# Output product in two row tiles with a drain per chunk, column-tile work gathered in one stretch, MLP work spread over head pairs

## The chip, the cores and the metric

One core of one Trainium2 chip. The metric is device time in microseconds (us), the median of several executions; the profiler took one execution of each kernel. "Span" is the profiled execution's time from its first to its last instruction; it is about 2 us shorter than the device time. A run is called slow when it is over 1.5% above the fastest of its kernel, else fast. Ratios use fast runs alone; a median that includes a slow run is marked.

## The reference

```python
# q, k, v: (8, 12, 448, 64) float32
scores = q @ k.T / 8 - log(448)
attn   = sigmoid(scores)                  # no softmax
x      = (attn @ v) -> (8, 448, 768)
wq, wk = x @ w_q, x @ w_k                 # 768 -> 64
mixed  = (wq @ wk.T / 8) @ x              # token mixing; the kernel does wq @ (wk.T @ x)
out    = relu(mixed) @ w_out              # (8, 448, 768) float32
```

## The kernel before

The unit of work is a "head pair" `n`: two batches and two heads (`u` is the batch pair, `j` the head pair in it; 4 x 6 = 24 pairs). ScalarE has seven sigmoids of 128 x 896 per pair. TensorE transposes q, k and x, makes scores and value products, and carries the MLP of the batch pair before along with it. The order inside a pair is written by hand:

```python
    for n, (u, j) in enumerate(pairs):
        ...                                   # loads, casts
        left = {0: 2, 1: 1}.get(j, 2 * (NJ - j) + (2 if u < NU - 1 else 0))
        tr_q(n + 1)                           # column tiles (128 rows x 64 columns)
        scores_last(n)                        # column tiles
        tr_k(n + 1)                           # column tiles
        tr_x(n - 2)                           # column tiles
        if u > 0 and j == 1:
            mlp_wkn(u - 1)
        scores(n, 0); scores(n, 1)            # row tiles (64 rows x 128 columns)
        whole(left)                           # output chunks, the whole 128 x 128 array
        scores(n, 2); scores(n, 3)            # row tiles
        values(n - 1, 0); values(n - 1, 1)    # column tiles
        if u > 0 and j == 1:
            mlp_tmp(u - 1)
        scores(n, 4); scores(n, 5)            # row tiles
        if u > 0 and j == 0:
            mlp_wqk(u - 1)
        elif u > 0 and j == 1:
            for c in range(NC):
                mlp_mix(u - 1, c)
            outs += outs_of(u - 1)            # 14 chunks
        else:
            whole(left - 1)
```

An output chunk is six accumulating matmuls over the whole array, then one copy out of PSUM:

```python
    def mlp_out(u, m, nb):
        ps = ps_f.tile([P, NB], F32, tag="f", name="po")       # NB = 384
        for c in range(NC):                                    # NC = 6
            nc.tensor.matmul(
                ps, mxs[u][c]...[:, m * P : (m + 1) * P],
                wout16[:, c, nb * NB : (nb + 1) * NB],
                start=(c == 0), stop=(c == NC - 1),
            )
        nc.vector.tensor_copy(out=ot[0][:, nb * NB : (nb + 1) * NB], in_=ps)
```

PSUM: two score tiles of two banks each, and four single banks ("f") for everything else.

## Time and profile before

| | before |
|---|---|
| device time, median (lowest to highest of 3) | 250.95 us (250.38 to 251.14) |
| span | 248.5 us |
| busy: TensorE / ScalarE / VectorE | 87% / 69% / 53% |
| mean granted TensorE clock | 0.981 |
| first sigmoid starts | 9.7 us |
| first stage ends (first sigmoid of pair 6) | 52.8 us |
| last sigmoid ends | 219.2 us |

### The profile page before, as it was taken

The numbers are of one execution on the slowest core, as the hardware profiler recorded it, in microseconds if no ns is written. First come the engines' busy times: TensorE is split into PE (matmuls) and PEld (weight loads), VectorE is DVE, ScalarE is ACT, GpSimd is POOL, SyncE is SP. The second block draws the span as 40 slices with busy tenths as digits, with TensorE's granted clock in tenths as the row PEclk, the third lists the DMA queues.
The fourth block names the chain that finished last, engine by engine and source line by source line (L and its number), as shares of the span: only waits on it lengthen the run. The fifth ranks groups of instructions, "written<-read, shape, count | busy, mean of one in ns | idle before, by whom it ended". The sixth has DMA issues, their size and how long they took to land.

```text
span 248.5 us, 6124 instructions
## 1 busy us (share of the span) xinstructions
PE 215.9 (87%) x2480; PEld 116.7 (47%) x2480; DVE 132.2 (53%) x230; ACT 171.7 (69%) x194; POOL 75.5 (30%) x84
## 2 busy tenths in 40 slices
PE   0878777779779999999979999999979999998992
PEld 0534334445435644545544554455444554453660
DVE  2423444454575555564685654655684564458551
ACT  2499889986677768986688678895698678724000
POOL 1655466566302131441633041343631010000000
PEclk9979999999979999999999999999999999999997
DMA  6999999999900498789872489789962543220376
GB/s 239 303 286 268 249 330 318 308 296 262 247 2 21 115 275 231 187 231 286 224 216 65 114 240 263 211 234 259 234 170 66 130 105 95 67 63 3 79 201 163
DMA packets 35387, 47.58 MB, mean 191 GB/s; under 512 B 6432, under 2 KB 31008, under 8 KB 35360
## 3 DMA queue, kind: packets, MB, share of 16 engines
q1 hardware_dynamic: 35088, 46.74, 70.2%
q8 instruction: 19, 0.31, 0.6%
q10 hardware_dynamic: 272, 0.46, 0.5%
q14 instruction: 8, 0.07, 0.1%
HBM read 36.18 MB, written 11.01 MB: 190 GB/s over the span
## 4 chain that ended last, share of the span: by engine, by line
PE 72%; ACT 17%; issue 5%; DVE 2%; DMA 2%; ACTq 0%
PE po L289 19%; PE pv L203 16%; ACT at L169 15%; PE sc L187 12%; PE ptk L155 5%; PE ptq L139 5%; PE sc L177 5%; PE px L223 4%; PE pw L236 4%; ACT mx L280 2%; PE pt L263 2%; DMA q<-in_q_dram 2%; PE pm L275 1%; DVE tmp L268 1%; PE pk L251 1%
## 5 line engine op out<-in xcount | busy, mean ns | idle before, releaser
L169 ACT ACTIVATE at<-sc,bias_t 128x896 bf16<-128x896 f32 x168 | 158.8, 1006 | 49.3 <-PE sc L177 23.7
L289 PE MATMUL po<-wout,mx 128*128 128x384 bf16 x336 | 59.6, 327 | 0.1
L187 PE MATMUL sc<-qt,kt 64*128 64x448 bf16 x288 | 47.2, 358 | 14.4 <-ACT at L169 14.0
L294 DVE COPY o<-po 128x384 f32<-128x384 f32 x56 | 31.2, 558 | 37.7 <-PE po L289 36.6
L207 DVE CAST xt<-pv 128x448 bf16<-128x448 f32 x48 | 30.0, 625 | 39.6 <-PE pv L203 36.4
L289 PEld LDWEIGHTS <-mx 128*128 128x128 bf16 x336 | 30.6, 98 | 25.2 <-issue 7.2
L203 PE MATMUL pv<-at,v 128*64 128x448 bf16 x384 | 40.9, 356 | 0.0
L116 POOL CAST q<-q 128x896 bf16<-128x896 f32 x23 | 21.5, 933 | 59.0 <-DMA q<-in_q_dram 29.9
L125 POOL CAST v<-v 128x1024 bf16<-128x1024 f32 x24 | 25.0, 1040 | 38.4 <-PE pv L203 21.0
L187 PEld LDWEIGHTS <-kt 64*128 64x128 bf16 x288 | 12.3, 93 | 43.3 <-issue 40.8
L116 POOL CAST k<-k 128x896 bf16<-128x896 f32 x24 | 22.6, 940 | 24.5 <-DMA k<-in_k_dram 16.9
L203 PEld LDWEIGHTS <-v 128*64 128x64 bf16 x384 | 19.7, 109 | 17.0 <-issue 6.1
L159 DVE COPY kt<-ptk 128x1024 bf16<-128x1024 bf16 x24 | 16.6, 690 | 9.7 <-PE ptk L155 9.7
L139 PE MATMUL ptq<-ident,q 128*64 128x128 bf16 x336 | 15.5, 238 | 6.0 <-DVE q L116 6.0
L143 DVE COPY qt<-ptq 128x896 bf16<-128x896 bf16 x24 | 15.0, 624 | 8.6 <-PE ptq L139 8.5
L139 PEld LDWEIGHTS <-q 128*64 128x64 bf16 x336 | 11.3, 119 | 14.2 <-issue 6.5
L280 ACT ACTIVATE mx<-pm 128x448 bf16<-128x448 f32 x24 | 11.7, 550 | 8.1 <-PE pm L275 8.0
L155 PEld LDWEIGHTS <-k 128*64 128x64 bf16 x336 | 15.1, 120 | 4.2 <-issue 0.8
L224 DVE COPY xn<-px 128x1024 bf16<-128x1024 bf16 x24 | 16.4, 681 | 0.4 <-PE px L223 0.4
L177 PE MATMUL sc<-qt,kt 128*64 128x448 bf16 x96 | 14.5, 382 | 2.2 <-ACT at L169 2.2
L155 PE MATMUL ptk<-ident,k 128*64 128x128 bf16 x336 | 16.4, 233 | 0.0
L279 DVE TENSOR_SCALAR mx<-pm 128x448 bf16<-128x448 f32 x24 | 13.8, 619 | 2.6 <-PE pm L275 2.4
(36 smaller groups left out, 125.5 us busy)
## 6 DMA issues: line engine op xcount, KB each, us to landing
q<-in_q_dram SPq DMA_DIRECT2D x24, 448.0 KB, 5.9
out_dram<-o SPq DMA_DIRECT2D x56, 192.0 KB, 2.7
k<-in_k_dram SPq DMA_DIRECT2D x23, 448.0 KB, 7.0
v<-in_v_dram SPq DMA_DIRECT2D x48, 128.0 KB, 6.0
v<-in_v_dram SPq DMA_DIRECT2D x48, 96.0 KB, 5.6
w<-in_moe_w_out_dram SPq DMA_DIRECT2D x6, 384.0 KB, 6.2
k<-in_k_dram ACTq DMA_DIRECT2D x1, 448.0 KB, 4.9
wqk<-in_moe_w_q_dram SPq DMA_DIRECT2D x2, 192.0 KB, 6.4
```

The source lines that it names most:

```text
L116: eng.tensor_copy(out=t16.rearrange("p b i d -> p b (i d)"), in_=ld.pop((nm, n)))
L125: nc.gpsimd.tensor_copy(out=t.rearrange("p b h s d -> p (b h s d)"), in_=v32[n % NV].rearrange("p b h s d -> p (b h s d)"),)
L139: nc.tensor.transpose(ps[HALF[b2], i].rearrange("p h n -> p (h n)"), t16[:, b2, i, :], ident16)
L155: nc.tensor.transpose(ps[HALF[b2], pos].rearrange("p h n -> p (h n)"), src, ident16)
L169: nc.scalar.activation(at, sc[:, :, 0:S], ACTF.Sigmoid, bias=bias_t, scale=attn_scale)
L177: nc.tensor.matmul(sc[HALF[b2], h, 0:S], kts[n][:, h, 3 * P + 64 * b2 : 3 * P + 64 * b2 + 64], qts[n][:, h, :], start=True, stop=True,)
L187: nc.tensor.matmul(sc[:, b2, 0:S], kts[n][HALF[b2], h, m * P : (m + 1) * P], qts[n][HALF[b2], h, :], start=True, stop=True,)
L203: nc.tensor.matmul(ps[HALF[b2]], v16s[n][:, b2, h, slot, :], rhs, start=(m == 0), stop=(m == 3))
L207: nc.vector.tensor_copy(out=t, in_=ps)
L280: nc.scalar.activation(mxs[u][c][:, 1, :], ps[1], ACTF.Relu, bias=0.0, scale=moe_scale)
L289: nc.tensor.matmul(ps, mxs[u][c].rearrange("p b s -> p (b s)")[:, m * P : (m + 1) * P], wout16[:, c, nb * NB : (nb + 1) * NB], start=(c == ...
L294: nc.vector.tensor_copy(out=ot[0][:, nb * NB : (nb + 1) * NB], in_=ps)
```

## The change

The intent: score matmuls use TensorE in two row tiles of 64 rows. If the output product does so too, scores and output can alternate without a change of tiling mode, in small "slots" between the score tiles. All work in column tiles is gathered in one stretch at the start of a pair, so a pair changes mode twice and not seven times. Upper and lower half of a chunk add into the same PSUM bank, so the upper half runs seven slots behind the lower one and a drain stands between them. The mix steps of the MLP are spread over three head pairs. The head of the program (warm-up matmuls, casts and copies in halves) and the tail (`wqk` begun early, copies shared with ScalarE) are reworked too. The diff is shortened: `...` marks cuts, and guards such as `if n > 0` and the placing of the small MLP transposes are left out.

```diff
+    LAG = NC + 1
+    def out_mm(n, c, x, last):                      # x: 0 lower half, 1 upper half
+        if x == 0 and c == 0:
+            state[n] = bank([P, NB], F32, "po")
+        r = HALF[x]
+        if x == 1 and c == 0:
+            nc.tensor.drain()
+        nc.tensor.matmul(
+            state[n][1], mxs[u][c]...[r, m * P : (m + 1) * P],
+            wout16[r, c, nb * NB : (nb + 1) * NB],
+            start=(x == 0 and c == 0), stop=(x == 1 and c == NC - 1),
+        )
...
+    def out_slot(last=False):
+        if s < end:
+            out_mm(s // NC, s % NC, 0, last)
+        if 0 <= s - LAG < end:
+            out_mm((s - LAG) // NC, (s - LAG) % NC, 1, last)
...
+        tr_q(n + 1); tr_k(n + 1)
+        scores_last(n)
+        values(n - 1, 0); values(n - 1, 1)
+        tr_x(n - 2)
...
+        mixes = ((1, (0, 1, 2, 3, 4, 5)),) if u == 1 else ((1, (0, 1)), (2, (2, 3)), (3, (4, 5)))
...
+        if u == 0:
+            for g in range(first, 6):
+                scores(n, g)
+            continue
+        scores(n, 0)
+        scores(n, 1)
+        gaps = [5, 5, 4, 4]
+        for g in range(2, 6):
+            fill(todo, gaps[g - 2])                  # slots, wqk or mix steps
+            scores(n, g)
```

## The prediction

> **What bounds the kernel now.** I read the busy slices first, then the chain of work that ended last, in order of time, then the timeline of TensorE, and last the groups by line. The page's busy rows, in 40 slices of 6.2 us:
>
> ```profile
> PE   0878777779779999999979999999979999998992
> ACT  2499889986677768986688678895698678724000
> ```
>
> There are three stages. Up to about 52 us (the six head pairs of the first batch pair) ScalarE is the fuller engine. From 52 to 218 us TensorE is at nine tenths or more. From 218 us TensorE works alone. The chain gives each stage its price. A pair of the first stage, one of the second, and the tail:
>
> ```profile
> 30.43 0.57 PE sc L177 x4
> 37.65 0.57 PE sc L177 x4
> ...
> 83.21 0.51 PE ptq L139 x14
> 84.55 0.45 PE px L223 x16
> 84.99 0.63 PE sc L187 x4
> 85.62 2.06 PE po L289 x12
> 87.68 0.48 PE sc L187 x4
> 88.17 1.64 PE pv L203 x16
> 89.80 0.60 PE sc L187 x4
> 90.40 2.06 PE po L289 x12
> 92.46 0.51 PE ptq L139 x14
> ...
> 220.58 2.42 PE pw L236 x24
> 229.85 13.82 PE po L289 x84
> 243.70 0.56 DVE o L294
> ```
>
> The first two lines are the same work one pair apart: 37.65 - 30.43 = 7.22 us. The pair from 83.21 to 92.46 takes 9.25 us and is TensorE from end to end. The output product of the last batch pair is 84 matmuls in 13.82 us, 0.1645 each, just over the 0.160 us that 384 columns take when 448 take 0.187 (the 24 matmuls of `pw`, below). From the same chain I took the starts of all pairs: a batch pair of the steady stage (107.75 to 162.63 us) costs 54.9 us, as 8.8, 12.25, 9.25, 9.25, 7.65, 7.65. Eighteen pairs run from 52.1 to 218.5 us: 166.4. The tail takes 30 us, of which 11.35 come before the first output product and 4.8 after the last.
>
> ScalarE, in the timeline of the first stage:
>
> ```profile
> 29.38 6.56 ACT L169 ACTIVATE at<-sc,bias_t 128x896 bf16<-128x896 f32 x7 [0.65 <-PE sc L187]
> 34.49 1.70 PE L203 MATMUL pv<-at,v 128*64 128x448 bf16 x16
> 36.12 0.55 PE L187 MATMUL sc<-qt,kt 64*128 64x448 bf16 x4
> 36.59 1.91 ACT L169 ACTIVATE at<-sc,bias_t 128x896 bf16<-128x896 f32 x2 [0.65 <-PE sc L187]
> ```
>
> Two sigmoids take 1.91 and one takes 1.01 us, so a sigmoid follows the other after 0.90 us, and seven need 6.3 us. The hole of 0.65 us is the value product: 1.7 us of TensorE during which only two score tiles, all that its buffers hold, can wait for ScalarE.
>
> **What the Trainium skill says.** (1) "TensorEngine Tiling (Array Packing)", Key Properties: "Changing tiling mode (not just tile) drains the TensorE". The trace agrees and gives the size: four score matmuls in row tiles are 2 x 0.187 = 0.37 us but cost 0.48 after the output product, the value product is 8 x 0.187 = 1.50 but costs 1.64, 14 transposes are 0.39 but cost 0.51. A change of mode is 0.11 to 0.14 us. (2) The same page, Gotcha 1: different row tiles may not access one PSUM bank simultaneously. That is why the upper half of an output chunk must come after the lower; no run here shows what happens otherwise. (3) "TensorE: Matmul & The Clock Gate", Part 3, row and column tiling: matmuls in different row groups run concurrently. Agrees: the 24 `pw` matmuls, two row tiles in turns, took 2.27 us in the body's chain, 0.189 a pair. (4) "PSUM — Partial Sum Buffer", Engine vs sequencer instructions: a drain waits until the engine is fully idle. The trace has TensorE's closing drain: it ends at 243.71, when VectorE's last copy starts (243.70); the last matmul started at 243.34 and streamed for 0.16 until 243.50. So a drain holds for at least 0.21 us beyond the stream.
>
> **The change part by part.**
>
> *Row tiles for the output.* One 128-row matmul of 384 columns becomes two of 64 rows in two row tiles. They run side by side, so a slot (one lower, one upper) is about 0.162 us: TensorE time neither gained nor lost, 336 matmuls more. The gain is that output and scores share one mode. Before, a pair with four output chunks changes mode seven times, afterwards twice: 5 x 0.12 = 0.6 us.
>
> *The drain.* There are 56, one per chunk. Each lets the array empty (0.21 us, above) and the next weights and matmul be issued from an empty queue, which I put at 0.07: D = 0.28 us, an estimate. The two lanes pair up again after it (upper k with lower k+1), so nothing else is lost. Three chunks per pair: 0.84 us, more than the 0.6 saved.
>
> *One column stretch.* TensorE in a pair: transposes 0.51 + 0.45 + 0.45, last scores 0.375, values 1.50 = 3.28 us; about 0.1 for banks, because two of the four are held by open output chunks; change of mode 0.12; six score tiles 6 x 0.187 = 1.12. Sum 4.6. With 18 slots: 4.6 + 18 x 0.162 + 0.84 = 8.4 to 8.5. But ScalarE now has one hole per pair: from the last score tile, values (1.5), a transpose (0.45), a mode change (0.12) and one score pair with its latency (0.36) lie before the next, 2.43 us, of which two sigmoids less the start cover about 1.1. So a pair bound by ScalarE takes 6.3 + 1.35 = 7.65 to 7.8, not 7.2.
>
> *Spread of the slots.* I counted in the built order. Pairs 8 to 11, 16, 17, 22, 23 hold (about) 18 slots; 12 and 18 hold 6 and the `pw` work; 14, 15 and 21 few or none but two mix steps (0.9 us of ScalarE); 36 of the last-but-one batch pair's 84 are done when the body ends. So 48 + 7 slots stand in the tail, where ScalarE has nothing to do. Before, none were left.
>
> *Pair 1 of each batch pair.* The small transposes of `wqk` now come first, right behind the copies of `pw`: TensorE stands about 1.2 us, then works through 5 us of column tiles over two free banks. I get 6.9 us before the first score, then 5: 11.7 to 12.3, like 12.25 before.
>
> *Head.* Warm-up matmuls, k cast by two engines, halves of the copies: first sigmoid at about 7.9 rather than 9.68; but the second pair's k lands and is cast as late as before (9.5), and it now stands ahead of the last scores of pair 0. Gain 1.3 us.
>
> Sum: head -1.3. Five pairs without MLP, +0.45 each: +2.2. Body: 7.8 + 12.3 + 8 x 8.45 + 2 x 8.2 + 11.7 + 12.1 + 3 x 8.65 + 8.9 = 162.8 against 166.4: -3.6. Tail: 55 + 91 slots x 0.162 + 23 drains x 0.28 = 30.1 against 13.8: +16.3; `wqk` begun early and copies shared with ScalarE -1.4; shorter last transfer -0.4. Total 250.95 - 1.3 + 2.2 - 3.6 + 14.5 = 262.8. Some drains will fall into waits for ScalarE or a bank and cost nothing; I take 2 to 4 us off: 259.
>
> **The rivals.**
>
> *The drain is cheap* (0.12, as a mode change): 56 x 0.16 = 9 us less, 250 to 254, no change. For it: the array empties at a mode change too, for 0.12. Against it: the closing drain's 0.21[...].
>
> *The even spread pays.* If pairs of 18 slots run at ScalarE's pace and its hole closes (7.2 us instead of 8.45, eight of them), 10 us go, and with a cheap drain the time is about 240. For it: pairs of 9.25 and 7.65 us stand side by side now, and TensorE is mostly waiting for nothing else. Against it: the mean of those four is 8.45 already, and the long column stretch makes ScalarE's hole larger, not smaller.
>
> *Banks bind harder.* Open output chunks hold two of four banks (three for a moment), so every transposition waits for VectorE's copy (0.62 to 0.69 us each, five a pair, plus 0.56 for each chunk). VectorE is near 55% now. If each of 5 stretches waits 0.2 instead of 0.1 in all, 18 x 0.9 = 16 us more: 270 and above. Against it: by my timing the copies end just before the bank is asked for.
>
> **Range and chances.** D between 0.12 and 0.35 moves 56 drains by -9 to +4 us; the pairs' sum may be off by 4 us either way. Around 259 this gives 249 to 268 for 8 in 10. Under 245.9 (faster by 2%) both first rivals must hold in part: 0.08. 245.9 to 256: 0.24. Slower: 0.68.
>
> **What would show it.** In the profile of the changed kernel: the start-to-start of matmuls across a drain (0.44 us if right, 0.28 if the first rival is); the spacing of pairs 8 to 11 (8.4, all alike); sigmoid holes of 1.2 us or more in every pair of the first stage and pairs 7.7 us apart there; output slots after the last scores taking about 11 us, and the last 84 chunks' matmuls about 18 to 19 instead of 13.8; the first sigmoid near 7.9. The prediction is wrong if the tail after the last scores stays near 30 us or if pairs of 18 slots take under 8 us.

## More of the kernel before

One more row of the page, which the prediction did not use, is the clock that TensorE was granted in each of the 40 slices, in tenths of full speed:

```profile
PEclk9979999999979999999999999999999999999997
```

Apart from the last slice, two are under full speed.

## The result, and the profile after

The changed kernel takes 276.07 us (275.08 to 278.99, four runs) against 251.04 us (four runs): a ratio of 1.1008, 95% interval 1.0914 to 1.1103. Ratios here are the mean time of one kernel's fast runs over that of the other's in the same rounds, so not quite the ratio of the medians. The prediction said 259, at most 268.

I took the start of each pair's first sigmoid from ScalarE's timeline of both kernels and cut the two spans into the same three stages:

| stage | before, us | predicted change | after, us | measured change |
|---|---|---|---|---|
| head and pairs 0 to 5 | 52.8 | +0.9 | 57.75 | +4.9 |
| pairs 6 to 23 | 166.4 | -3.6 | 170.7 | +4.3 |
| tail, after the last sigmoid | 29.3 | +14.5 | 44.5 | +15.3 |
| sum | 248.5 | +11.8 | 273.0 | +24.5 |

The tail's sum came as worked out. Over a third of the loss (9.2 of 24.5 us) is in the other two stages, and there the sum was wrong. The rows of the page after (TensorE, ScalarE, granted clock):

```profile
PE   7668766688689999989867999998998999989993
ACT  3785887857688877783896697656788785115111
PEclk9997979979999999999979799999999999999997
```

In the first ten slices TensorE, mostly at 7 or 8 before, is at 6 to 8; ScalarE, mostly at 8 or 9 before, is at 5 to 8 after the first slice; and the clock row has five slices at 7, apart from the last, instead of two.

First, the drains. The chain of the tail, with start and duration:

```profile
251.49 1.15 PE po L346 x12
252.63 0.11 issue
252.74 1.15 PE po L346 x12
253.90 0.11 issue
254.00 1.15 PE po L346 x12
```

Twelve half matmuls (six slots) follow each other after 252.74 - 251.49 = 1.25 us (1.26 on average over the tail's chunks). Six slots alone are 6 x 0.162 = 0.97 us. A drain costs 0.28 to 0.29 us, as estimated. The sign that the prediction named agrees: from one lower half to the next it is 0.163 us inside a chunk and 0.44 us across a drain.

Second, a pair of 18 slots, in the chain (some lines between are left out):

```profile
95.58 0.38 PE sc L200 x4
95.96 1.51 PE pv L226 x16
97.48 0.60 PE px L247 x16
98.80 0.98 PE po L346 x9
100.28 0.82 PE po L346 x7
102.41 0.65 PE po L346 x8
103.25 0.51 PE ptq L148 x14
104.35 0.38 PE sc L200 x4
```

104.35 - 95.58 = 8.77 us, TensorE from end to end; 8.4 to 8.5 was predicted. Some 0.2 us of the difference is in the column stretch: 3.59 us from the first transpose to the first row-tile score, where 3.28 and 0.1 for banks was worked out.

Third, the first stage, in the timeline (start, duration; in brackets how long the engine stood before and what released it):

```profile
22.51 2.65 PE L226 MATMUL pv<-at,v 128*64 128x448 bf16 x16
26.00 6.50 ACT L192 ACTIVATE at<-sc,bias_t 128x896 bf16<-128x896 f32 x7 [2.24 <-PE sc L210]
31.29 1.68 PE L226 MATMUL pv<-at,v 128*64 128x448 bf16 x16
33.81 5.50 ACT L192 ACTIVATE at<-sc,bias_t 128x896 bf16<-128x896 f32 x6 [1.31 <-PE sc L210]
```

The same value product takes 2.65 us in one pair and 1.68 in the next, and ScalarE stands 2.24 us before the one and 1.31 before the other. Nothing in the program differs. The view by windows shows why; its columns are the stretch, its length, busy time and instructions of TensorE, its weight loads, VectorE, ScalarE and GpSimd, then the granted clock, the DMA share and GB/s:

```profile
17.63:21.04 3.41, 1.81 (x26) 0.81 (x27) 0.00 (x0) 3.41 (x5) 1.12 (x2) 1.00 1.07 303
21.04:24.45 3.41, 3.41 (x36) 2.05 (x32) 1.52 (x3) 1.97 (x3) 1.97 (x2) 0.50 1.07 203
34.70:38.11 3.41, 1.64 (x17) 0.63 (x18) 0.00 (x0) 3.41 (x5) 2.98 (x4) 1.00 1.07 351
38.11:41.52 3.41, 3.41 (x41) 2.28 (x38) 1.32 (x2) 2.20 (x3) 1.63 (x3) 0.50 1.07 303
147.34:150.75 3.41, 1.67 (x10) 0.50 (x10) 1.12 (x3) 3.41 (x6) 0.00 (x0) 1.00 0.00 0
150.75:154.16 3.41, 3.40 (x40) 2.44 (x41) 1.55 (x3) 2.50 (x4) 1.81 (x2) 0.50 0.00 0
```

The clock is granted in windows of 3.41 us. The five windows at half clock in this kernel, apart from its last microseconds, each follow a window in which TensorE was busy for 1.4 to 1.9 of 3.41 us (1.81, 1.64 and 1.67 in the fence). This is no sharp threshold: the half-clock window at 71.84 us in the kernel before follows a window with 2.25 us of work, and in some runs a window with 1.8 to 2.2 us was followed by full clock. Gathering the column-tile work made just such windows: first some 3.6 us in which TensorE issues one score tile per 0.9 us and otherwise waits, then 3.3 us of dense work, which in every second pair begins at half clock.

### The profile page after: what moved, and what is told of

Read it like the earlier page. It is cut to its first block, busy times and chain, and to the rows that moved or that the text cites. A ratio compares the mean times of both kernels' runs of the same rounds, so it can differ in the third digit from the quotient of the medians.

```text
span 273.0 us, 6949 instructions
## 1 busy us (share of the span) xinstructions
PE 230.9 (85%) x2852; PEld 131.5 (48%) x2852; DVE 126.5 (46%) x218; ACT 177.9 (65%) x209; POOL 74.9 (27%) x84
## 4 chain that ended last, share of the span: by engine, by line
PE 74%; ACT 12%; issue 7%; DVE 4%; POOL 0%; ACTq 0%; POOLq 0%
PE po L346 24%; PE pv L226 14%; ACT at L192 10%; PE sc L210 9%; PE ptk L171 5%; PE ptq L148 5%; PE px L247 5%; PE sc L200 4%; PE pw L262 3%; PE pt L295 2%; ACT mx L309 2%; DVE wqk L272 2%; PE pwarm L418 1%; PE pm L319 1%; DVE mx L311 1%
## 5 line engine op out<-in xcount | busy, mean ns | idle before, releaser
L346 PE MATMUL po<-wout,mx 64*128 64x384 bf16 x672 | 81.0, 324 | 6.7 <-DVE mx L311 1.3
L210 PE MATMUL sc<-qt,kt 64*128 64x448 bf16 x288 | 55.3, 354 | 22.2 <-ACT at L192 21.7
L346 PEld LDWEIGHTS <-mx 64*128 64x128 bf16 x672 | 36.0, 94 | 46.9 <-issue 32.3
L361 DVE COPY o<-po 128x384 f32<-128x384 f32 x44 | 24.5, 557 | 53.4 <-PE po L346 52.4
L230 DVE CAST xt<-pv 128x448 bf16<-128x448 f32 x48 | 30.0, 624 | 19.7 <-PE pv L226 16.9
L226 PEld LDWEIGHTS <-v 128*64 128x64 bf16 x384 | 25.9, 116 | 14.7 <-issue 5.1
L154 DVE COPY qt<-ptq 128x896 bf16<-128x896 bf16 (+1 forms) x25 | 15.1, 605 | 37.7 <-PE ptq L148 36.8
L134 POOL CAST v<-v 128x1024 bf16<-128x1024 f32 x24 | 25.0, 1040 | 23.6 <-DMA v<-in_v_dram 10.3
L359 ACT COPY o<-po 128x384 f32<-128x384 f32 x12 | 5.7, 478 | 22.9 <-PE po L346 22.7
L311 DVE TENSOR_SCALAR mx<-pm 128x448 bf16<-128x448 f32 x24 | 14.6, 622 | 11.1 <-PE pm L319 9.5
L177 DVE COPY kt<-ptk 128x1024 bf16<-128x1024 bf16 (+1 forms) x25 | 16.6, 666 | 1.9 <-PE ptk L171 1.6
L247 PEld LDWEIGHTS <-xt 128*64 128x64 bf16 x336 | 13.2, 109 | 5.4 <-issue 3.5
L319 PE MATMUL pm<-wqk,tmp 64*128 64x448 bf16 x48 | 13.0, 348 | 3.2 <-ACT mx L309 2.2
L200 PE MATMUL sc<-qt,kt 128*64 128x448 bf16 x96 | 15.5, 400 | 0.3 <-ACT at L192 0.3
```

The costliest lines, as they stand in the source:

```text
L134: nc.gpsimd.tensor_copy(out=t.rearrange("p b h s d -> p (b h s d)"), in_=v32[n % NV].rearrange("p b h s d -> p (b h s d)"),)
L200: nc.tensor.matmul(sc[HALF[b2], h, 0:S], kts[n][:, h, 3 * P + 64 * b2 : 3 * P + 64 * b2 + 64], qts[n][:, h, :], start=True, stop=True,)
L210: nc.tensor.matmul(sc[:, b2, 0:S], kts[n][HALF[b2], h, m * P : (m + 1) * P], qts[n][HALF[b2], h, :], start=True, stop=True,)
L226: nc.tensor.matmul(ps[HALF[b2]], v16s[n][:, b2, h, slot, :], rhs, start=(m == 0), stop=(m == 3))
L230: nc.vector.tensor_copy(out=t, in_=ps)
L247: nc.tensor.transpose(ps[HALF[par], m, :, h, :], src, ident16)
```

## The experiments

I had three theories for the part that the prediction missed. *Clock*: the half-clock windows. *Drains*: they cost their full 0.28 us everywhere, and the discount of 2 to 4 us was wrong. *Banks*: open chunks hold PSUM banks that other work needs. Against them stood the rival that the order itself (one long column stretch) starves ScalarE, whatever the clock. The device times below are medians of four runs if not said otherwise, beside runs of the kernel before on the same chip (250.9 to 251.4 us); the diffs are shortened. A plain removal of the drain (two row tiles writing one bank with nothing to order them) was not run.

### Two banks instead of the drain (a1_two_banks)

```diff
-        if x == 1 and c == 0:
-            nc.tensor.drain()
-            state[n] = bank(...)                       # one bank per chunk, lag of 7
+            state[n, x] = bank(...)                    # a bank for each half, no lag
+        nc.vector.tensor_tensor(out=dst, in0=ps1, in1=dst, op=ALU.add)
```

> The changed kernel with lower and upper half of a chunk in two PSUM banks, no lag and no drain; VectorE copies one and adds the other (0.6 us more per chunk). Theory 'each of the 56 drains costs its 0.29 us on the path': the 23 drains of the tail give back 6.7 us, the 33 of the body most of 9.6, so 12 to 16 us less, about 260 to 264 us, pairs of 18 slots from 8.76 to about 8.0 us. Rival 'in the body the drains fall into waits': only the tail gains, about 269 us, pairs of 18 slots stay near 8.7.

Measured: 273.6 us, only 2.5 less, and neither theory's number. The timeline of the tail says where the drains went (two chunks per line):

```profile
232.21 2.13 PE L344 MATMUL po<-wout,mx 64*128 64x384 bf16 x24 [0.17 <-DVE o L361]
232.43 0.56 DVE L361 TENSOR_TENSOR o<-po,o 128x384 f32<-128x384 f32 x1 [0.27 <-ACT o L357]
234.51 2.13 PE L344 MATMUL po<-wout,mx 64*128 64x384 bf16 x24 [0.17 <-DVE o L361]
```

Two chunks come every 2.30 us, 1.15 each instead of 1.26: TensorE now waits for VectorE's second copy to free a bank. In pairs of 18 slots (8.57 us) ScalarE's sigmoids in the row stretch come down to 0.89 us apart, which is its own pace, and the holes around the last score tile remain. The profiled run also lost 2.3 us more than the changed kernel by pair 6, to the clock. So removing the drain this way puts another wait in its place; it does not tell what the drain costs.

### A second drain per chunk (b3_double_drain)

```diff
-        if x == 1 and c == 0:
+        if x == 1 and c in (0, 3):
             nc.tensor.drain()
```

> The changed kernel with a second drain in each chunk, before the fourth upper matmul. If a drain costs 0.29 us wherever TensorE is the bound: the tail's 23 give 6.7 us, and the body's 33 nearly all of 9.6, since pairs of 18 slots are TensorE's (8.76 to about 9.6): 290 to 292. If ScalarE bounds the body: the tail alone, 283.

Measured: 291.3 us, 15.2 more for 56 more drains: 0.27 us each at most, for in the profiles 1.25 of the 15.2 us fall in the first stage, which has no drains, and its clock windows differ. The tail grew from 44.5 to 50.4 (23 drains, 0.26 each), pairs 6 to 23 from 170.7 to 178.7 (33 drains, 0.24 each); pairs 9 to 11 grow from 8.76 to 9.50 us (three drains, 0.25 each). So the body pays for a drain nearly what the tail pays, where nothing can hide it. The discount in the prediction was wrong.

### Whole-array output in the new order (a2_whole)

```diff
-        r = HALF[x];  drain;  LAG = NC + 1
+        r = slice(0, P)                                # one matmul of 128 rows per slot, no lag
```

> The changed kernel with the output as whole-array matmuls again (one per slot, no lag, no drain), order and slots otherwise unchanged. Theory 'row tiles pay 0.6 us of mode changes and cost 0.87 of drains': here a pair of 18 slots has eight more mode changes of 0.12 (about 1 us) and no drain (0.87 less), so 8.8 to 9.0 us, no gain in the body; the tail loses 23 drains and 7 lag slots (6.7 + 2.2 us): about 267 us. Rival 'row tiles with drains are the main loss in the body too': pairs of 18 slots under 8.3 us and under 262 us in all.

Measured: 264.1 us (the median of four runs, one of them slow), 12.0 less than the changed kernel. Pairs of 18 slots take 8.44 us, between the two theories (8.8 to 9.0, and under 8.3). The starts of the matmuls show three parts: three drains went (-0.84 us), eight changes of mode came back at 0.10 each (+0.8), and the column stretch takes 3.30 us instead of 3.59, as its transposes no longer wait: in the changed kernel the transposes of k stand until VectorE has copied a chunk out of its bank. The third part was in neither theory. The tail falls from 44.5 to 37.4, a little less than the 8.9 expected. So without row tiles the new order still loses 12 to 13 us against the kernel before (the ratio is 1.0485).

### The old order, with row tiles and without (b1_old_order, b2_old_order_whole)

Both keep the changed kernel's head, tail and helpers, and put the work of each pair back in the order of the kernel before. The first keeps row tiles, lag and drains, the second has whole-array matmuls.

```diff
-        tr_q; tr_k; scores_last; values; tr_x; scores and slots
+        tr_q; scores_last; tr_k; tr_x; scores 0, 1; chunks; scores 2, 3; values; scores 4, 5; chunks
```

> The changed kernel's row tiles, lag, drains, head and tail, but with the work of each pair in the order of the kernel before (value products between score tiles 3 and 4, whole chunks at the old places). If order and spread are the larger part of the loss: pairs of the first stage 7.1 to 7.3 us, no slots left for the tail except the lag; the row tiles then cost only the drains (0.29 each; 14 in the tail 4.1 us plus 1.1 of lag, some 5 in the body), less 2 to 3 of head and last transfer: about 258. If row tiles and drains are the larger part: over 265.

> As the run of the old order, with whole-array output matmuls: what is left of the change is its head (warm-up, split casts and copies) and its tail (wqk begun early, ScalarE's copies, split last transfer). If they are gains of their own: 2.2 us at pair 1 and 0.8 at the end, about 248 us. If the loads or the clock take the head's gain back: 251.

Measured: 277.05 us with row tiles, 253.5 with whole-array matmuls (one of its four runs slow). Together with the two runs in the new order:

| | whole-array output | row tiles and drains | row tiles cost |
|---|---|---|---|
| old order | 253.5 | 277.05 | 23.5 |
| new order | 264.1 | 276.1 | 12.0 |
| new order costs | 10.6 | -1 | |

The two parts are not additive. With whole-array output the new order costs 10.6 us. With row tiles it costs nothing more, because in the old order row tiles run into something that the new order avoids. It is in the second head pair of a batch pair: 17.0 and 17.2 us for pairs 13 and 19, 12.4 and 12.8 with whole-array output. The view of the `pm` tile (the mix steps' PSUM tile) in the old order with row tiles, what its engines waited for (us, times):

```profile
  PE pm L319: 13.2, 26
  ACT mx L309: 7.2, 12
  DVE mx L311: 1.5, 4
```

TensorE waits 7.2 us for ScalarE's copies of the mix steps: there are four banks, two are held by open chunks, so one mix step fills the other two and the next must wait.

The second run also answers for the head. Pair 1 starts at 14.6 us instead of 16.9, but pair 2 at 23.55 instead of 23.96, and the window view has the reason:

```profile
14.24:21.06 6.82, 5.75 (x44) 2.67 (x39) 1.64 (x3) 5.12 (x6) 2.91 (x3) 0.50 1.08 308
```

Two windows at half clock: the head's gain of 2.3 us was given back by pair 2.

### Chunks closed before the mix steps (d1_closed_chunks)

```diff
+            while out_slot(flush=True):                # the last upper halves now
+                pass
             for c in range(NC):
                 mlp_mix(u - 1, c)
```

> The run of the old order with row tiles and drains, but the last upper halves of a batch pair's chunks are issued before the mix steps, so that no open chunk holds a PSUM bank there. If the 17 us of the second head pairs 13 and 19 (12.4 and 12.8 with whole-array matmuls) come from banks held by open chunks: both fall to 12.5 to 13.5 and the time by 7 to 9 us, to about 269; what is left over the whole-array run (253.5) is then 56 drains of 0.27, 15 us. If they come from the drains or the order: no change, 277.

Measured: 270.5 us, 6.5 less. Pairs 13 and 19 fall to 14.9 and 15.0 (they now contain the closing of the chunks, and the pairs after them are 1.1 shorter). The same view of `pm`:

```profile
  PE pm L319: 3.2, 11
  DVE mx L311: 1.7, 8
  ACT mx L309: 1.1, 1
```

The wait for ScalarE's copies fell from 7.2 to 1.1 us. Held banks are shown as a cost of row tiles with a lag, and they explain two thirds to three quarters of the 9 us that these two pairs lost. Part of that comes by way of the clock: the stretch at half clock at each of these pairs shrank from 6.83 to 3.41 us. The rest over whole-array output, 270.5 - 253.5 = 17.0 us, is about what 56 drains (0.25 to 0.28 each, 14 to 16 us) and the lag come to; no run separates these.

### All mix steps early (c1_early_mix, c2_early_mix_whole)

55 slots were left when the scores ended. With all mix steps in the second head pair of each batch pair the slots start two pairs earlier and 19 are left.

```diff
-        mixes = ((1, (0, 1, 2, 3, 4, 5)),) if u == 1 else ((1, (0, 1)), (2, (2, 3)), (3, (4, 5)))
+        mixes = ((1, (0, 1, 2, 3, 4, 5)),)
```

> The changed kernel with all six mix steps of a batch pair in its second head pair (as it has for the first only), so that the slots of the next chunks start two pairs sooner and 19 instead of 55 slots are left when the scores end. If slots in the tail cost their full time and slots in the body lie in time that ScalarE's pace leaves: 36 x 0.162 and 6 or 7 drains less, 7 to 9 us: about 268. If they only move: the pairs that take them grow from 9.7 and the time stays within 2 us.

Measured: 277.0 us (its profiled run, at 279.4, is slow; the three others are fast). The tail fell by 7.4 us, from 44.5 to 37.1, as expected, but pairs 13 and 19 rose from 10.3 and 11.7 to 15.2 and 15.5. My expectation overlooked the banks. The same change with whole-array output, where a chunk holds one bank and none at its end:

> The changed kernel with all mix steps in the second head pair, and whole-array output matmuls (an open chunk then holds one bank and none at a chunk's end). If held banks made that run's pairs 13 and 19 slow (15.2 and 15.5 us): here about 12.5 each, the tail some 5 us shorter than with whole-array matmuls alone, and the time 257 to 260. If early mixing itself does not pay: 264 as with whole-array matmuls alone.

Measured: 257.9 us (one of four runs slow), pairs 13 and 19 at 11.5 each, tail 31.6. So spreading the mix steps was not a gain of its own: it was needed because row tiles hold banks, and it pushed 36 slots into the tail, where ScalarE has nothing to do.

### TensorE kept busy in the first stage (a3_dummies)

```diff
             for g in range(first, 6):
                 scores(n, g)
+                if 1 <= g < 5 and n > 0:
+                    dummy(n, 4)        # 4 pairs of row-tile matmuls that nobody reads
```

> The changed kernel with four pairs of throw-away row-tile matmuls after the score tiles 1 to 4 of pairs 1 to 5, so that TensorE does not stand in the first stage. Theory 'the granted clock': the clock of 20 to 60 us goes from 0.83-0.92 to 1.00 and the pairs there from 8.75 to about 7.7 us (ScalarE's 6.3 and a hole of 1.3): 5 us less, about 271. Rival 'the order alone makes the hole': pairs stay near 8.7 us, same time.

Measured: 273.2 us, 2.9 less. The clock of the first stage, after and with dummies:

```profile
14.50:57.00 42.50, 29.71 (x374) 17.13 (x372) 14.93 (x25) 32.71 (x36) 23.56 (x26) 0.90 1.03 286
```

```profile
14.50:57.00 42.50, 39.98 (x578) 24.98 (x574) 17.46 (x29) 35.15 (x39) 23.87 (x26) 1.00 1.04 283
```

TensorE was given 10 us more work and finished sooner: pairs 2 to 5 take 7.82 us each instead of 8.5 to 9.0. Pair 6 starts 4.2 us earlier. Some of that is given back in pair 7, where two windows at half clock fell in this run. 7.82 is what the prediction worked out for a pair bound by ScalarE's hole (7.65 to 7.8): the hole was sized rightly, the clock was missing.

### The value products out of the stretch (a4_split_values)

```diff
+                if g == 3 and n > 0:       # u == 0 only
+                    values(n - 1, 0)
+                    values(n - 1, 1)
```

> The changed kernel with the value products of pairs 1 to 5 back between the score tiles 3 and 4 of the pair, out of the column stretch. Both 'hole' and 'clock' theories: ScalarE's holes shrink to about 0.65 us and TensorE's work is spread, so clock near 1.00 and pairs of 7.2 to 7.4 us instead of 8.75: 6 to 8 us less, about 269. A rival 'the first stage is bound by the loads': pairs stay above 8.3 us.

Measured: 270.5 us (one of four runs slow), 5.6 less. Pairs 3 to 5 take 7.05 us, a little less than before (7.21); pair 2 took 8.3, with a half-clock window at its end. The loads are not the bound. With the run before: of the 1.5 us by which a first-stage pair grew (8.75 against 7.21), about 0.95 is the clock and 0.6 the longer hole.

### The clock elsewhere (d2_clock_held, d3_clock_bursts)

Pairs 14 and 15 take 9.7 us each; I had worked out 8.65. Both runs put dummies there too, the first one per empty slot, the second four pairs in each of four gaps.

> The changed kernel with throw-away matmuls wherever TensorE has slots without work: pairs 1 to 5 as in the run before with them, and the empty slots of pairs 6, 7 and 13 to 15. If the half-clock windows are what the first stage and pairs 14 and 15 lost: the clock is 1.00 from pair 1 to the end, pairs 1 to 5 take 7.8 us, 14 and 15 about 8.7 instead of 9.7 each, and 6 to 7 us go, about 269 to 270. If the dummies cost as much as the clock gives, or the windows only move, 273 as before.

Measured: 293.1 us. A failed experiment: each dummy took two of the four banks anew and had to wait for them, so pairs 13 to 15 took 16.4, 14.6 and 13.9 us, and windows at half clock came all the same.

> The run with throw-away matmuls in pairs 1 to 5, and four more pairs of them in each of the four gaps of pairs 14 and 15, in one burst per gap that takes its two banks once (the run before took two banks for every one and waited for each). If the half-clock window at the start of the column stretches of pairs 15 and 16 is what those pairs lose: clock 1.00 from 139 to 160 us, pairs 14 and 15 about 8.7 to 8.9 us each instead of 9.7, about 271 us against 273 with dummies in the first stage alone. If ScalarE's mix steps make them long: 9.6 as before, 273.

Measured: 273.4 us, the same as with dummies in the first stage alone. The clock was 1.00 from 132 to 165 us, yet the pairs took 9.9 and 10.5. The starts of single sigmoids split this: the last interval before the next pair fell from 1.94 and 1.96 to 1.28 and 1.42 us, which I take for what the clock gave back, since the half-clock windows had stood there, but the intervals between the score tiles rose from 0.89 and 1.31 to 1.25 to 1.58 because the dummies stood in front of them. So by this reading, not by a shorter time, about 0.6 us of each of these pairs is the clock; the rest (0.4) was not taken apart.

### A version from what the runs showed (e1_best, e2_best)

Old order, whole-array output, head and tail of the change, dummies in pairs 0 and 1 alone, and the mix steps of the second head pair between its score tiles instead of behind them:

```diff
+        mlp_tmp(u - 1)                                 # j == 1: right after scores 0, 1 and the chunk
         scores(n, 2)
+        mlp_mix(u - 1, 0); mlp_mix(u - 1, 1)
         scores(n, 3)
+        mlp_mix(u - 1, 2)
         values(n - 1, 0); values(n - 1, 1)
         scores(n, 4)
+        mlp_mix(u - 1, 3)
         scores(n, 5)
+        mlp_mix(u - 1, 4); mlp_mix(u - 1, 5)
```

> A version put together from what the runs showed: order of the kernel before, whole-array output matmuls, the changed kernel's head and tail, throw-away matmuls in pairs 0 and 1 so that the clock stays full there, and the second head pair's mix steps between its score tiles instead of behind them. If the half clock took the head's gain back: pair 2 starts at 22 instead of 23.5 us, worth 1.5 to 2. If the mix steps' 12.4 us are TensorE waiting for copies, the three pairs fall to about 11: 3 to 4 us. Together about 247 to 248; if neither holds, 252 to 253.

Measured: 246.6 us, ratio to the kernel before 0.9806 (0.9766 to 0.9847): faster than both kernels, though whether by 2% is unclear. The clock row of its page has no slice under 9:

```profile
PEclk9999999999999999999999999999999999999999
```

Pairs 7, 13 and 19 take 11.2, 11.6 and 11.6 us instead of 13.2, 12.3 and 12.3. Pair 2 starts at 22.1 instead of 23.96.

> The best version, with the transposes of k ahead of the last score tile in pairs 1 to 5, as they stood in the run with the value products split out, where these pairs took 7.05 us instead of 7.27. If it is that order: 1 us less, about 245.5; if that came from elsewhere: 246.6.

Measured: 247.65 us (six runs), no gain. Pairs 2 to 4 did take 7.05 us, but in the profiled run a half-clock window fell in pair 5 (8.25). The clock alone does not explain it: the two runs with a clock of 0.999 and 1.0 took 246.06 and 246.26 us, no faster than the runs of e1_best (246.17 to 247.29).

## Why the prediction was wrong

**The direction was right, and so was the larger term.** The tail was to grow by 14.5 us (55 left slots, 23 drains of 0.28); it grew by 15.3. That this sum came out so near is in part luck. In the chain the output took 11.2 us after the last scores and 18.0 for the last batch pair, 29.2 where 30.1 was worked out, and the kernel before also had 1.1 us of output after its last scores, which the sum left out; the last transfer gained 0.8 and not 0.4 us. Against that the steps between the two (238.62 to 250.99) took 12.4 us, where 11.35 - 1.4 was forecast: the gain from an earlier `wqk` and shared copies did not come. The drain was sized at 0.28; the tail shows 0.28 to 0.29 and the double drain about 0.25. The first rival, a cheap drain, is refuted. The second, that the even spread pays, is refuted: pairs of 18 slots take 8.76 us.

**The step that failed first: "Five pairs without MLP, +0.45 each: +2.2"** (with the head +0.9 in all; measured +4.9). Pair 1 started 2.2 us earlier, and pairs 1 to 5 took 7.1 us more (43.05 instead of 35.9). The mechanism, ScalarE's hole, was right (7.82 us with a full clock; with dummies the five pairs take 2.65 us more than before), but the sum took every TensorE duration at full clock. The page's clock row was there to read, and the kernel before already had two slices under 9. The runs showed in its place: stretches in which TensorE was busy about half the time were followed by 3.41 us at half clock, and the change made one such stretch in every two pairs, so a pair took 8.5 to 9.0 us.

**The second: "Some drains will fall into waits ...; I take 2 to 4 us off."** Next to none did. Doubling them cost 0.24 each in the body against 0.26 in the tail, so about half a microsecond was hidden, and three more in a pair bound by TensorE lengthened it by 0.74 of the 0.84 us.

**The third, and the largest: the body's sum, 162.8 us; measured 170.7.** Of the miss of 17 us it makes 7.9, the first stage 4.0, the discount 3.8, the tail 0.8. By its terms:

| pairs | predicted | measured |
|---|---|---|
| 8 to 11, 16, 17, 22, 23 | 67.6 | 68.7 |
| 6 and 7 | 20.1 | 21.3 |
| 12 and 13 | 19.9 | 20.9 |
| 14 and 15 | 17.3 | 19.4 |
| 18 and 19 | 20.3 | 22.4 |
| 20 and 21 | 17.55 | 18.0 |

Pairs 14 and 15 lost some 1.2 us of their 2.1 to the clock, by the reading of d3_clock_bursts. For the pairs with `wqk` and mix steps, the third rival, that banks bind harder, was named with the right cause and mostly at the wrong place: the column stretch stands 0.2 us longer than worked out in a pair of 18 slots, but more is lost at `wqk` and the mix steps, which want two banks at once. Pairs 18 and 19 show it. With whole-array output in the same order (a2_whole) they take 19.5 us; with what a second drain cost in them (0.26 and 0.51 us) that is 20.3, the predicted figure. In the changed kernel they take 22.4, and TensorE stands 0.55 us before the second bank of `wqk`, until VectorE has copied a chunk, and 0.65 and 0.24 us before output matmuls, until VectorE has copied a mix step: 1.44 of the 2.1 us. None of these three waits is in a2_whole. These pairs ran at full clock in both runs. The other two such rows, too, lost their 1.0 and 1.2 us at full clock; no run takes them apart.

**Smaller misses.** The head's first sigmoid came at 8.3 (7.9 predicted), pair 1 started 2.2 us earlier (1.3 predicted), but by pair 2 most of it was gone. With the old order and whole-array output the reworked tail is 30.1 us against 29.3 before, so it was no gain there either. Pair 21 held 10 slots, not "few or none". And "TensorE is at nine tenths or more" from 52 to 218 us overlooked four slices at 7: the pairs with all mix steps, 7, 13 and 19, the same that e1_best shortened.

## What to carry to other kernels

Here a change of tiling mode cost 0.10 to 0.14 us; before saving it at the price of a drain, put the drain's 0.25 to 0.29 us and the PSUM banks that half-done accumulations hold beside it. An engine that is not the bound can still be slowed by its own slackness: gathering TensorE's dense work into one burst after a stretch at half load made the burst run at half clock in every second pair; spreading it (5.6 us, with a shorter hole for ScalarE) or a little useless work (2.9 us) won part of the loss back. Read the clock row of the page before using any TensorE duration, and ask of work moved to a tail whether anything else runs there.

## What the Trainium skill lacked or had wrong

- "TensorE: Matmul & The Clock Gate", HAM oscillation and the table of goals: the rule given is to have no TensorE-idle gaps of more than about 3 us. In the changed kernel no gap was longer than 0.6 us within the five windows that were followed by half clock; TensorE was busy for 1.4 to 1.9 of 3.41 us there. The page's next subsection does say that frequent short idles can bring half clock, but gives no length and no share. The window of 3.41 us that the page gives is confirmed: the half-clock windows are 3.41 or 6.83 us long.
- "TensorEngine Tiling (Array Packing)", Key Properties: a change of mode drains the array, but no cost is given. Here it is 0.10 to 0.14 us.
- "PSUM — Partial Sum Buffer", Engine vs sequencer instructions: a drain waits for the engine to go idle, but no cost is given. Here it is 0.25 to 0.29 us of TensorE time each, paid nearly in full.
- "TensorEngine Tiling (Array Packing)", Gotcha 1 (PSUM pressure) speaks of banks written at the same time. No page speaks of banks held over time by a lagging half, beyond a general advice to evacuate promptly: two of four here, and with the mix steps 7.2 us of waiting for copies against 1.1 when the chunks were closed first.
